# An attention and mixture-of-experts kernel: the whole program as a graph that a list scheduler orders, and a cosine without absolute value

## The chip, the cores and the metric

The kernel runs on one core of one Trainium2 chip. The metric is the device time of one execution in microseconds; of several executions the median counts. The core has five queues that matter here: TensorE (PE in the rows; its weight loads are PEld), VectorE (DVE), ScalarE (ACT), GpSimd (POOL) and SyncE (SP), which issues the DMAs.

## What is computed

Three stages follow one another: attention with keys and values pooled by 8, a dense layer pair with g = h·cos(h), and a mixture of 8 experts whose gate is normalised in 8 Sinkhorn rounds.

```python
def _moe_ref(x, w_in, w_out):
    h = x @ w_in                      # x 2304x512, w_in 512x2048
    g = h * np.cos(h)
    return (g @ w_out).astype(np.float32)

def _moe2_ref(x, w_gate, w1, w2):
    ...                               # P: 2304x8, 8 rounds of row and column sums
    for e in range(E):                # 8 experts, w1 512x1024, w2 1024x512
        h = np.maximum(x @ w1[e], 0.0)
        ye = h @ w2[e]
        out += P[:, e:e + 1] * ye
```

The two weights of the dense pair reach the kernel as 64-bit floats, two 32-bit words each, and become 32-bit floats on the chip.

## The kernel before

Every matmul operand is split into a high half in the reduced format fp32r and the low remainder, and each product is three matmuls: high·high, high·low, low·high (`mm3`). ScalarE writes the high half as a copy; VectorE or GpSimd subtracts it for the low half. What GpSimd can take is a choice of the code, engine by engine.

**Attention and the dense pair (0 to about 540 us).** The 2304 tokens are six blocks of 384 (NB), in the groups [0..3] and [4, 5]; the 2048 hidden columns are four units of 512. `hidden1` (L374 to L392) makes one hidden tile of 128x384: 12 matmuls into the bank `ph`, then ScalarE rounds h/2π to an integer k (L384), VectorE forms r = h - 2πk (L385), ScalarE takes |r| (L387) and sin(π/2 - |r|) (L388), VectorE multiplies by h (L389), ScalarE copies the high half gh (L391), and GpSimd (first group) or VectorE (second) subtracts for gl (L392). 96 such tiles are made. `output1` (L395) multiplies by w_out and adds to `acc` in SBUF (L416, L418); from it come the high and low halves of the next input (L420, L421).

In the first unit `convert` (L108) makes 32 pieces of 128x512 from the 64-bit words: an absolute value on ScalarE (L118), five operations on VectorE (L119 to L127), the add on GpSimd (L128, `cw`); it stores the 32-bit result, and `split` (L93) halves it. For other units and the second group `load_unit` (L100) loads the 32-bit weights, 512 KB a time, and splits them anew: a ScalarE copy (L96) and a GpSimd subtraction (L97) each. The pooling sums of keys and values (`kr`, `ks`, `vr`, `vs`, L202 and L204) stand on GpSimd, except for the first batch; the softmax is on VectorE (L299, L336, L337) and ScalarE. The order of this part follows from that in which the code stands, with lists of attention and conversion tasks worked off between the tiles.

**Mixture of experts (from about 540 us).** Two blocks of tokens make a pair; there are three pairs, and 16 steps (8 experts, two halves of 512 columns each) per pair. The first layer of a step is always a Strassen-Winograd product in two half steps of seven products, P1, P5, P6, P2, P7, P3, P4 (`first_layer` L864, matmuls at L860, six of 384 columns each). Its banks are px (P1, then P2), pv (P5, then P3) and py: when py has been read, ScalarE copies P1's result into it (L879), and P6, P7 and P4 add to it. In pair 0 the second layer is plain (`plain_layer`, L1015, groups of 24 matmuls of 256 columns, `po`), while GpSimd, VectorE and ScalarE form the weight pieces of the Strassen products (L639 to L771) and store them. In pairs 1 and 2, 32 steps, the second layer is Strassen-Winograd too (`strassen_layer`, L1033, banks pc and qc). Its left operands come from `strassen_result` (L912): per half step a sum `spare` on VectorE (L961), three differences `sf` on GpSimd (`combine`, L638), and for seven operands the halves gh (ScalarE) and gl (VectorE). `accumulate` (L993) weighs the result with the gate and adds it (`acc`, L1011). P4 of the second layer may only be added to a qc bank when VectorE has read it (L1066).

The order here is written out by hand: strings such as `"aa0a1a0a1a0a..."` set TensorE's sequence (a: a first-layer product; L or a digit: a piece of the second layer), and a plan with allowances (`later`, `tick`, `until`) puts the other engines' work between. SyncE's DMAs are not in that order.

Of the kernel before, what the change touches and what calls it, by code (L numbers as in the profile page):

```python
# [56 lines left out]

@with_exitstack
def fused_kernel(ctx: ExitStack, tc: tile.TileContext, qT, kT, vT, v0, wa1, wb1, wa2, wb2, wg, out):
    nc = tc.nc  # L60

    const = ctx.enter_context(tc.tile_pool(name="const", bufs=1))
    xp = ctx.enter_context(tc.tile_pool(name="xp", bufs=1))
    wp = ctx.enter_context(tc.tile_pool(name="wp", bufs=19))
    gfirst = ExitStack()
    rawp = gfirst.enter_context(tc.tile_pool(name="rawp", bufs=3))
    gp = gfirst.enter_context(tc.tile_pool(name="gp", bufs=6))
    banks = ExitStack()
    ps_h = banks.enter_context(tc.tile_pool(name="ps_h", bufs=2, space=bass.MemoryType.PSUM))
    ps_o = banks.enter_context(tc.tile_pool(name="ps_o", bufs=2, space=bass.MemoryType.PSUM))  # L70
    ps_s = banks.enter_context(tc.tile_pool(name="ps_s", bufs=2, space=bass.MemoryType.PSUM))
    ps_a = banks.enter_context(tc.tile_pool(name="ps_a", bufs=2, space=bass.MemoryType.PSUM))


# [3 lines left out]
    ident = const.tile([P, P], F32, name="ident")  # L78
    make_identity(nc, ident)


    marks = {}

    @contextmanager
    def behind(engine):
        if engine in marks:
            with tc.issue_after(marks[engine].ins):
                yield
        else:
            yield  # L90


    def split(src, lo_engine, pool=None):  # L93
        hi = (pool or wp).tile([P, FU], F32R, tag="w", name="whi")
        lo = (pool or wp).tile([P, FU], F32R, tag="w", name="wlo")
        nc.scalar.activation(out=hi, in_=src, func=AF.Copy)  # L96
        lo_engine.tensor_tensor(out=lo, in0=src, in1=hi.bitcast(F32), op=ALU.subtract)  # L97
        return hi, lo

    def load_unit(src, u, lo_engine):  # L100
        parts = []
        for j in range(2):
            raw = rawp.tile([P, 2, FU], F32, tag="raw", name="raw")
            nc.sync.dma_start(out=raw, in_=src[u, :, 2 * j:2 * j + 2, :])
            parts += [split(raw[:, i, :], lo_engine) for i in range(2)]
        return parts

    def convert(raw, keep, u, j):  # L108

        words = raw.bitcast(I32).rearrange("p (n w) -> p n w", w=2)  # L110
        high, low = words[:, :, 1], words[:, :, 0].bitcast(U32)
        m = cv.tile([P, FU], I32, tag="m", name="m", bufs=2)
        w = cv.tile([P, FU], F32, tag="cw", name="cw", bufs=2)
# [12 lines left out]
        v.tensor_scalar(out=w.bitcast(I32), in0=m, scalar1=-2**23, scalar2=None, op0=ALU.bitwise_and)
        v.scalar_tensor_tensor(out=w, in0=low, scalar=2.0**-52, in1=w, op0=ALU.mult, op1=ALU.mult)  # L127
# [1212 lines left out]
```

## Time and profile before

| | |
|---|---|
| three runs, us | 2015.01, 2014.88, 2011.66; median 2014.88 |
| profiled execution, us | 2012.12, span 2010.4, granted clock 0.99 |
| TensorE busy | 1955.4 us, 97% of the span, 13220 matmuls |
| VectorE, ScalarE, GpSimd busy | 67%, 49%, 38% |
| chain that ended last | TensorE 67% |
| HBM traffic | 317 MB read, 134 MB written |

The profile shows one execution. A busy share is an average over stages that differ; so it is read by windows, each with the engines' busy time in it and TensorE's granted clock as a share of its full 2.4 GHz. A group of instructions is a line, an engine, an operation and a tile, with the mean time of one. A wait names what ended it.

### The profile page before, as it was taken

The numbers are of one execution on the slowest core, as the hardware profiler recorded it, in microseconds if no ns is written. First come the engines' busy times: TensorE is split into PE (matmuls) and PEld (weight loads), VectorE is DVE, ScalarE is ACT, GpSimd is POOL, SyncE is SP. The second block draws the span as 40 slices with busy tenths as digits, with TensorE's granted clock in tenths as the row PEclk, the third lists the DMA queues.
The fourth block names the chain that finished last, engine by engine and source line by source line (L and its number), as shares of the span: only waits on it lengthen the run. The fifth ranks groups of instructions, "written<-read, shape, count | busy, mean of one in ns | idle before, by whom it ended". The sixth has DMA issues, their size and how long they took to land.

```text
span 2010.4 us, 36447 instructions
## 1 busy us (share of the span) xinstructions
PE 1955.4 (97%) x13220; PEld 1917.9 (95%) x13220; DVE 1354.3 (67%) x2282; ACT 988.4 (49%) x2133; POOL 765.2 (38%) x643
## 2 busy tenths in 40 slices
PE   6799999999989999999999999999999999999999
PEld 4689899999989999999999999999999999999999
DVE  8988776655587676676765566666667656656665
ACT  5676566655534344444434444444445444444443
POOL 7755654432574454344442222122124222212212
PEclk8899999999999999999999999999999999999999
DMA  7533431211688888889897677677668767767763
GB/s 252 153 125 116 126 121 53 83 54 45 222 290 292 310 305 302 298 300 310 306 315 260 236 266 257 229 258 272 232 237 285 245 238 273 248 233 259 268 226 120
DMA packets 257460, 453.33 MB, mean 225 GB/s; under 512 B 25568, under 2 KB 86752, under 8 KB 257280
## 3 DMA queue, kind: packets, MB, share of 16 engines
q1 hardware_dynamic: 257280, 451.01, 65.8%
q8 instruction: 104, 1.70, 0.3%
q14 instruction: 76, 0.62, 0.1%
HBM read 317.21 MB, written 133.69 MB: 224 GB/s over the span
## 4 chain that ended last, share of the span: by engine, by line
PE 67%; DVE 2%; issue 1%; DMA 1%; POOL 1%; ACT 1%; SPq 0%; DVEq 0%; POOLq 0%; ACTq 0%
PE py L860 14%; PE pc L1043 13%; PE po L1025 11%; PE qc L1043 10%; PE pv L860 9%; PE px L860 9%; DMA raw<-wb 1%; DVE gl L646 1%; POOL t L639 0%; DVE vlo L646 0%; DMA w2c<-vhi 0%; POOL vlo L646 0%; DVE gl L840 0%; POOL wlo L646 0%; DVE acc L1011 0%
## 5 line engine op out<-in xcount | busy, mean ns | idle before, releaser
L639 POOL TENSOR_TENSOR sf<-spare 128x384 f32<-128x384 f32 x64 | 66.0, 1032 | 702.3 <-DVE spare L961 702.3
L1043 PE MATMUL pc<-wc,gh 128*128 128x256 f32 x1536 | 284.0, 280 | 0.0
L1043 PEld LDWEIGHTS pc<-wc,gh 128*128 128x128 f32 x1536 | 241.1, 188 | 0.0
L860 PE MATMUL py<-xc,wc 128*128 128x384 f32 x1152 | 232.2, 336 | 0.3 <-DVE pv L886 0.3
L1043 PE MATMUL pc<-wc,gl 128*128 128x256 f32 x768 | 215.6, 281 | 1.1 <-DVE gl L646 1.1
L1043 PE MATMUL qc<-wc,gh 128*128 128x256 f32 x1152 | 215.7, 280 | 0.2 <-DVE pc L1062 0.2
L860 PEld LDWEIGHTS py<-xc,wc 128*128 128x128 f32 x1152 | 193.1, 188 | 0.6 <-DVE pv L886 0.6
L1043 PEld LDWEIGHTS qc<-wc,gh 128*128 128x128 f32 x1152 | 191.6, 188 | 0.9 <-DVE pc L1062 0.6
L1043 PE MATMUL qc<-wc,gl 128*128 128x256 f32 x576 | 162.2, 282 | 0.4 <-DVE gl L646 0.4
L860 PE MATMUL pv<-xc,wc 128*128 128x384 f32 x768 | 155.3, 337 | 2.8 <-DVE gl L840 2.8
L1025 PE MATMUL po<-vlo,gh 128*128 128x256 f32 x768 | 153.0, 281 | 2.3 <-POOL vlo L646 2.3
L646 DVE TENSOR_TENSOR gl<-sf,gh 128x384 fp32r<-128x384 f32 x256 | 148.5, 619 | 9.8 <-ACT gh L652 9.8
L860 PE MATMUL px<-xc,wc 128*128 128x384 f32 x768 | 154.7, 336 | 0.0
L1025 PE MATMUL po<-vhi,gh 128*128 128x256 f32 x768 | 152.4, 280 | 0.0
L1025 PE MATMUL po<-vhi,gl 128*128 128x256 f32 x768 | 152.3, 280 | 0.0
L1043 PEld LDWEIGHTS pc<-wc,gl 128*128 128x128 f32 x768 | 145.1, 189 | 1.3 <-DVE gl L646 1.3
L137 PE MATMUL ph<-xh,whi 128*128 128x384 f32 x384 | 131.2, 346 | 5.9 <-DVE r L389 5.9
L860 PEld LDWEIGHTS pv<-xc,wc 128*128 128x128 f32 x768 | 130.6, 188 | 3.1 <-DVE gl L840 3.1
L138 PE MATMUL ph<-xl,whi 128*128 128x384 f32 x384 | 131.3, 342 | 0.7 <-DVE xl L370 0.7
L860 PEld LDWEIGHTS px<-xc,wc 128*128 128x128 f32 x768 | 130.7, 188 | 0.0
L886 DVE TENSOR_TENSOR pv<-py,s 128x384 f32<-128x384 f32 x96 | 54.2, 564 | 113.5 <-ACT gh L652 87.9
L138 PE MATMUL po<-gl,whi 128*128 128x384 f32 x384 | 129.5, 338 | 0.8 <-POOL gl L392 0.8
(206 smaller groups left out, 5162.8 us busy)
## 6 DMA issues: line engine op xcount, KB each, us to landing
wc<-w1c SPq DMA_DIRECT2D x448, 256.0 KB, 4.7
wc<-w2c SPq DMA_DIRECT2D x448, 256.0 KB, 5.3
w1c<-whi SPq DMA_DIRECT2D x112, 256.0 KB, 4.4
w1c<-wlo SPq DMA_DIRECT2D x112, 256.0 KB, 3.1
w2c<-vhi SPq DMA_DIRECT2D x112, 256.0 KB, 3.8
w2c<-vlo SPq DMA_DIRECT2D x112, 256.0 KB, 2.6
raw<-wa SPq DMA_DIRECT2D x48, 512.0 KB, 5.9
raw<-wb SPq DMA_DIRECT2D x48, 512.0 KB, 4.1
```

The costliest lines, as they stand in the source:

```text
L137: nc.tensor.matmul(out=ps, lhsT=lh, rhs=rh, start=(i == 0), stop=False)
L138: nc.tensor.matmul(out=ps, lhsT=lh, rhs=rl, start=False, stop=False)
L639: nc.gpsimd.tensor_tensor(out=out, in0=x, in1=y, op=op)
L646: e.tensor_tensor(out=lo(), in0=src, in1=high.bitcast(F32), op=ALU.subtract)
L860: nc.tensor.matmul(out=ps, lhsT=l[:, k], rhs=r[:, c, :], start=(start and c + n == 0), stop=(c + n == 3), skip_group_check=True)
L886: nc.vector.tensor_tensor(out=s["v"], in0=ps, in1=s["s5"], op=ALU.add)
L1025: nc.tensor.matmul(out=po[:, d * HD:(d + 1) * HD], lhsT=l[:, r], rhs=w[f % 2, d][k][:, (f // 2) * HD:(f // 2 + 1) * HD], start=(f + n + d ...
L1043: nc.tensor.matmul(out=ps, lhsT=l[:, r], rhs=m[:, k], start=(start and g + n == 0), stop=(g + n == 3), skip_group_check=True)
```

## The change

Every operation becomes a node of one graph: an engine (or two to choose from), planned microseconds, the buffers it reads and writes, and for matmuls a due time. A list scheduler walks through planned time and picks for each engine, among the nodes that could start first, the one whose due time is nearest; SyncE's DMAs are ordered in the same way. TensorE's due times in the experts' part come from the same strings as before.

```diff
-        marks["act"] = nc.scalar.activation(out=k, in_=ps, func=AF.Copy, scale=1.0 / (2.0 * math.pi))
-        nc.vector.scalar_tensor_tensor(out=r, in0=k, scalar=-2.0 * math.pi, in1=ps, op0=ALU.mult, op1=ALU.add)
-
-        nc.scalar.activation(out=r, in_=r, func=AF.Abs)
-        nc.scalar.activation(out=r, in_=r, func=AF.Sin, scale=-1.0, bias=math.pi / 2.0)
+        activate(NB, lambda: r.tile.bitcast(I32), ps, reads=[bank], writes=[r], from_psum=True,
+                 scale=1.0 / (2.0 * math.pi), bias=0.25)
+        add("V", two(NB), lambda: nc.vector.scalar_tensor_tensor(
+            out=r.tile, in0=r.tile.bitcast(I32), scalar=-2.0 * math.pi, in1=ps(), op0=ALU.mult, op1=ALU.add), [bank], [r])
+        activate(NB, lambda: r.tile, lambda: r.tile, AF.Sin, writes=[r], table="sin", bias=math.pi / 2.0)
...
-        nc.gpsimd.tensor_tensor(out=w, in0=mf, in1=w, op=ALU.add)
-        nc.sync.dma_start(out=keep[u, :, j, :], in_=w)
-        return w
+        tt(VG(FU), lambda: w.tile, mf, lambda: w.tile, ALU.add, [m], [w])
+        parts = [buf(k_w if u == 0 else k_cs, [P, FU], F32R, "wc") for _ in range(2)]
+        halves(FU, lambda: w.tile, w, lambda k: parts[k].tile, parts)
+        for k in range(2):
+            load(lambda k=k: wac[u, i, k], lambda k=k: parts[k].tile.bitcast(F32), P * FU * 4, reads=[parts[k]],
+                 writes=[kept_wa[u, i, k]])
+        return parts
...
+    def tt(how, out, in0, in1, op, reads, writes):
+
+        def run(e="V"):
+            (nc.gpsimd if e == "G" else nc.vector).tensor_tensor(out=out(), in0=in0(), in1=in1(), op=op)
+
+        return add(how["engine"], how["us"], run, reads, writes, port=how.get("port", False))
...
+            node.run(e) if len(node.engine) > 1 else node.run()
...
-    def combine(out, x, y, op):
-        nc.gpsimd.tensor_tensor(out=out, in0=x, in1=y, op=op)
-        return out
+        def gsum(out, x, y, reads, writes):
+            return tt({"engine": "G", "us": pool(NB), "port": True}, out, x, y, ALU.subtract, reads, writes)
...
-    with tc.manual_schedule(engines={E_.PE, E_.Activation, E_.DVE, E_.Pool}):
...
+    with tc.manual_schedule(engines={ENGINES.PE, ENGINES.Activation, ENGINES.DVE, ENGINES.Pool, ENGINES.SP}):
+        g.schedule()
```

- The rounding constant 0.25 moves k so that the sine's argument r + π/2 stays within its range without |r|: 96 ScalarE operations fewer.
- The converted weights are halved once and stored as two halves (64 stores of 256 KB in the place of 32), and loaded as halves (112 loads of 256 KB in the place of 28 of 512 KB); 32 ScalarE copies and 32 GpSimd subtractions fall away.
- `VG` marks operations that the scheduler may put on VectorE or on GpSimd: weight adds and low halves, pooling sums, gl, weight pieces. It plans so that a GpSimd operation and a VectorE operation marked `port` (operands in SBUF) don't overlap. The first copy to `acc` may be on ScalarE or VectorE. `hidden1` has three banks for `ph`.
- A node with one engine calls `run` without it, and `tt` then takes VectorE: so the `gsum` nodes, planned as GpSimd's, stand on VectorE.
- The matmuls are the same in number and size. VectorE has 2627 instructions instead of 2284, ScalarE 2004 instead of 2111, GpSimd 254 instead of 648, SyncE 1727 instead of 1595.

**GpSimd at the start**, from its first softmax product (`at`) on. Before:

```order
L299 TENSOR_TENSOR at<-at,rs 128x288
L128 TENSOR_TENSOR cw<-m,cw 128x512
L299 TENSOR_TENSOR at<-at,rs 128x288 x2
L202 TENSOR_TENSOR kr<-kr 128x288
L299 TENSOR_TENSOR at<-at,rs 128x288
L97 TENSOR_TENSOR wlo<-cw,whi 128x512
L202 TENSOR_TENSOR kr<-kr 128x288
L202 TENSOR_TENSOR kr<-kr 128x144
L202 TENSOR_TENSOR kr<-kr 128x288
L202 TENSOR_TENSOR kr<-kr 128x144
L204 TENSOR_TENSOR ks<-kr 128x72
```

Now:

```order
L449 TENSOR_TENSOR at<-at,rs 128x288
L449 TENSOR_TENSOR kr<-kr 128x288 x2
L449 TENSOR_TENSOR kr<-kr 128x144
L449 TENSOR_TENSOR ks<-kr 128x72 x3
L449 TENSOR_TENSOR vr<-vr 72x512 x3
L449 TENSOR_TENSOR vr<-vr 72x256 x2
L449 TENSOR_TENSOR vs<-vr 72x128 x2
L449 TENSOR_TENSOR vr<-vr 72x256
L449 TENSOR_TENSOR cw<-m,cw 128x512
L449 TENSOR_TENSOR vr<-vr 72x512
L449 TENSOR_TENSOR wc<-cw,wc 128x512
L449 TENSOR_TENSOR vr<-vr 72x256
```

Weight adds and low halves (`cw`, `wlo`) stood between the pooling sums; now the sums come first, and one `cw` and one low half (`wc`) stand among the first twelve rows. Up to the 430th matmul, seven of ten `cw` and five of ten low halves stand on VectorE.

**VectorE in a Strassen step**, from the sum `spare` of a half step on. Before:

```order
L961 SCALAR_TENSOR_TENSOR spare<-pv_17698,c_17802 128x384
L1011 SCALAR_TENSOR_TENSOR acc_12611<-qc,pr,acc_12611 128x512
L646 TENSOR_TENSOR gl<-spare,gh 128x384
L646 TENSOR_TENSOR gl<-c_17802,gh 128x384
L646 TENSOR_TENSOR gl<-sf,gh 128x384 x3
L886 TENSOR_TENSOR pv_17889<-py,s_17896 128x384
L646 TENSOR_TENSOR gl<-sf,gh 128x384
L1062 TENSOR_TENSOR pc<-qc,t_17923 128x256
L941 SCALAR_TENSOR_TENSOR gl<-px_17870,gh 128x384
```

Now (the lines are those of the changed kernel; L1209 is `spare`, L1251 `acc`):

```order
L1209 SCALAR_TENSOR_TENSOR spare<-pv_16153,c_16247 128x384
L449 TENSOR_TENSOR gl<-c_16247,gh 128x384
L449 TENSOR_TENSOR sf<-spare 128x384
L1251 SCALAR_TENSOR_TENSOR acc_12583<-pc,pr,acc_12583 128x512
L449 TENSOR_TENSOR qc<-qc,t_16207 128x256
L449 TENSOR_TENSOR sf<-spare,sf 128x384
L449 TENSOR_TENSOR gl<-spare,gh 128x384
L449 TENSOR_TENSOR gl<-sf,gh 128x384
L1251 SCALAR_TENSOR_TENSOR acc_12724<-qc,pr,acc_12724 128x512
L449 TENSOR_TENSOR sf<-sf 128x384
```

Three differences `sf` stand among them, the first two ahead of the next gl of `spare`; `acc` and the qc sum stand behind the first.

**TensorE at the start of a plain step**, from the first layer's second product (P5, bank pv) on. Before (left out: the rest of the 24 `po` matmuls):

```order
L860 MATMUL pv_8246<-xc,wlo 128x384
L1025 MATMUL po<-vhi,gh 128x256 x2
L1025 MATMUL po<-vlo,gh 128x256 x2
L1025 MATMUL po<-vhi,gl 128x256 x2
L1025 MATMUL po<-vhi,gh 128x256 x2
...
L1025 MATMUL po<-vhi,gl 128x256 x2
L860 MATMUL py<-xc,whi 128x384 x2
L860 MATMUL py<-xc,wlo 128x384
```

Now (L1148 are the first layer's matmuls):

```order
L1148 MATMUL pv_8216<-xc,whi 128x384 x2
L1148 MATMUL pv_8216<-xc,wlo 128x384
L1148 MATMUL pv_8216<-xc,whi 128x384 x2
L1148 MATMUL pv_8216<-xc,wlo 128x384
L1148 MATMUL py<-xc,whi 128x384 x2
```

The group of the second layer (`po`) that stood between P5 and P6 (py) has gone from there; P6 follows P5.

## Rows read from the trace of the kernel before

**Rows 1.** The windows view: window: us, busy us of each engine (instructions), clock, DMA.

```profile
30.00:130.00 100.00, 81.81 (x460) 69.66 (x459) 95.83 (x168) 64.60 (x111) 73.62 (x78) 0.88 0.52 160
130.00:500.00 370.00, 362.50 (x2108) 350.24 (x2107) 253.40 (x445) 224.92 (x450) 173.50 (x144) 1.00 0.26 85
500.00:605.00 105.00, 95.48 (x584) 92.38 (x583) 72.38 (x140) 48.45 (x98) 70.09 (x53) 0.97 0.75 253
600.00:1000.00 400.00, 399.65 (x2892) 399.04 (x2892) 282.04 (x410) 176.64 (x344) 181.50 (x130) 1.00 0.88 302
1030.00:1055.00 25.00, 21.83 (x151) 21.11 (x151) 18.83 (x20) 8.89 (x16) 16.65 (x8) 0.93 0.90 310
1050.00:1500.00 450.00, 449.70 (x3207) 449.39 (x3206) 274.27 (x478) 203.42 (x481) 100.04 (x90) 1.00 0.74 254
```

**Rows 2.** TensorE's waits, 30:130, 130:540 and 540:640: us, times, longest.

```profile
PE psc L279 <- DVE at L337: 6.0, 2, 5.6
...
PE ph L137 <- DVE r L389: 4.8, 6, 1.5
...
PE po L1025 <- POOL vlo L646: 2.3, 1, 2.3
```

**Rows 3.** GpSimd's groups by shape, 30:130: busy us, mean ns, idle before.

```profile
L128 POOL TENSOR_TENSOR cw<-m,cw 128x512 f32<-128x512 f32 x10 | 13.9, 1389 | 7.6 <-DVE cw L127 7.6
...
L202 POOL TENSOR_TENSOR vr<-vr 72x512 f32<-72x512 f32 x8 | 10.6, 1325 | 3.0 <-DMA vr<-vt 3.0
...
L204 POOL TENSOR_TENSOR ks<-kr 128x72 f32<-128x72 f32 x9 | 5.0, 560 | 0.1
```

**Rows 4.** VectorE's groups by shape, 30:130.

```profile
L299 DVE TENSOR_TENSOR at<-at,rs 128x288 f32<-128x288 f32 x20 | 17.5, 925 | 0.1
L123 DVE SCALAR_TENSOR_TENSOR m<-raw,m 128x512 int32<-128x512 int32 x10 | 10.3, 1039 | 0.0
...
L337 DVE TENSOR_TENSOR at<-psc,mx 128x288 f32<-128x288 f32 x20 | 8.6, 441 | 0.0
...
L126 DVE TENSOR_SCALAR cw<-m 128x512 int32<-128x512 int32 x10 | 7.3, 743 | 0.0
...
L119 DVE TENSOR_SCALAR m<-m 128x512 f32<-128x512 f32 x8 | 6.4, 800 | 0.1
L121 DVE TENSOR_SCALAR m<-m 128x512 int32<-128x512 int32 x8 | 6.4, 795 | 0.0
```

**Rows 5.** VectorE's groups by shape, 565:1040.

```profile
L646 DVE TENSOR_TENSOR wlo<-raw,whi 128x512 fp32r<-128x512 f32 x65 | 73.0, 1122 | 0.0
...
L646 DVE TENSOR_TENSOR wlo<-s,whi 128x512 fp32r<-128x512 f32 x26 | 17.7, 680 | 0.0
...
L1004 DVE TENSOR_TENSOR acc<-po,acc 128x512 f32<-128x512 f32 x6 | 4.1, 688 | 4.6 <-PE po L1025 4.6
...
L1149 DVE TENSOR_SCALAR acc<-acc,pr 128x512 f32<-128x512 f32 x6 | 2.5, 472 | 0.0
```

**Rows 6.** ScalarE's groups by shape, 0:565.

```profile
L387 ACT ACTIVATE r<-r 128x384 f32<-128x384 f32 x96 | 49.6, 521 | 37.4 <-DVE r L385 36.3
...
L384 ACT ACTIVATE r<-ph 128x384 int32<-128x384 f32 x96 | 46.1, 485 | 57.7 <-PE ph L139 54.7 <-POOL gl L392 2.6
```

**Rows 7.** VectorE's groups by shape, Strassen steps, 1100:1500.

```profile
L646 DVE TENSOR_TENSOR gl<-sf,gh 128x384 fp32r<-128x384 f32 x108 | 61.1, 605 | 4.2 <-ACT gh L652 4.2
L1011 DVE SCALAR_TENSOR_TENSOR acc<-pc,pr,acc 128x512 f32<-128x512 f32 x39 | 29.2, 750 | 10.4 <-PE pc L1043 10.4
...
L1066 DVE TENSOR_TENSOR qc<-qc,t 128x256 f32<-128x256 f32 x40 | 17.3, 432 | 3.0 <-PE qc L1043 0.2
...
L961 DVE SCALAR_TENSOR_TENSOR spare<-pv,c 128x384 f32<-128x384 f32 x28 | 15.6, 557 | 14.8 <-PE pv L860 14.8
```

**Rows 8.** TensorE's timeline from 1200 us: start us, us, instruction.

```profile
1201.23 1.21 PE L860 MATMUL py<-xc,wc 128*128 128x384 f32 x6
1202.28 0.40 PE L1043 MATMUL qc<-wc,gh 128*128 128x256 f32 x2
```

More of the change, by code (lines that the diff above doesn't have):

```diff
@@ L2 @@
 import struct
[L3 removed]
+from contextlib import ExitStack
 import concourse.bass as bass
@@ new lines, with __init__, __getitem__ @@
+class Kind:
+    def __init__(self, group, pool, slots, strict=False):
+        self.group, self.pool, self.slots, self.strict = group, pool, slots, strict
+        self.queue = []
+class Buf:
+    def __init__(self, kind, shape, dtype, name, tile=None):
+        self.kind, self.shape, self.dtype, self.name, self.tile = kind, shape, dtype, name, tile
+        self.acc, self.left, self.slot, self.end = [], 0, None, 0.0
+    def __getitem__(self, key):
+        return self.tile[key]
+class Node:
+    __slots__ = ("engine", "us", "run", "succ", "wait", "new", "bufs", "port", "table", "size", "goal", "late", "est", "slots",
+                 "end", "done", "name")
@@ L71, in fused_kernel @@
-    ps_s = banks.enter_context(tc.tile_pool(name="ps_s", bufs=2, space=bass.MemoryType.PSUM))
-    ps_a = banks.enter_context(tc.tile_pool(name="ps_a", bufs=2, space=bass.MemoryType.PSUM))
+    g = Graph(ctx, tc)
+    add, buf = g.add, g.buf
+    base = g.group("base")
+    first = g.group("first")
+    second = g.group("second")
+    early = g.group("early", "right")
+    mid = g.group("mid", "right", (early,))
+    late = g.group("late", "right", (second,))
+    plain = g.group("plain", "left", (second,))
@@ L193, in fused_kernel, with fill @@
[L193 to L206 removed]
+    def fill(b, hp, ks, ks_ap):
         kbd = kbds[b % 2]
@@ new lines, in fused_kernel, with prime @@
+    g1 = {}
+    x_op = x_pieces(0)
+    for j in range(NBLK):
+        logits(j, clock["t"] - 24.0 + 4.5 * j)
+    primes = [buf(b_y, [P, 512], F32, "pset"), *(buf(b_q, [P, 512], F32, "pset") for _ in range(2))]
+    def prime():
+        for t in primes:
+            nc.tensor.matmul(out=t.tile, lhsT=wg2[:, 0, :], rhs=wg2.tile.rearrange("p c n -> p (c n)"), start=True, stop=True)
+    node = pe(0.7, prime, [wg2], primes, goal=clock["t"] - 5.0)
+    for other in g.nodes:
+        if other is not node and any(b.kind in (b_a, b_o, b_s0) for b in other.new):
+            other.succ.append(node)
+            node.wait += 1
```

1884 lines of the change are left out of this document (965 added, 919 removed).

## Prediction

> **What bounds the kernel now.** I read first the windows by stage, since an average over the span mixes stages with different limits. From 600 us on TensorE is full: 399.65 of 400 us, and 449.70 of 450 in the Strassen steps, at granted clock 1.00 [rows 1]. No matmul is added or removed, so after 600 us the change can save next to nothing; it can only cost there. What can be saved lies in four places of the same view. From 30 to 130 us TensorE is busy for 81.81 of 100 us at clock 0.88: 18.2 us idle, and 81.8 x 0.12 = 9.8 us of low clock. From 130 to 500 us it idles 7.5 us, from 500 to 605 us 9.5 us and 95.5 x 0.03 = 2.9 us of clock, at 1030 to 1055 us 3.2 and 1.5 us [rows 1]. That is 52.6 us, and the clock falls only where TensorE also idles.
>
> Second, who is full where TensorE idles: from 30 to 130 us VectorE works 95.83 of 100 us [rows 1]. The chain of waits says the same: the score bank is awaited from VectorE's subtraction (6.0 us), then the bank ph of `hidden1` from the product r (4.8 us in six waits), then one low half from GpSimd (2.3 us) [rows 2]. So the start is VectorE's, and what the change puts on VectorE there counts in full.
>
> Third, what one operation costs on either engine. The add of a 128x512 weight is 1389 ns on GpSimd [rows 3]; VectorE's ops of that size on free ports are 680 to 688 ns with two inputs and 472 ns with one [rows 5]. The same ops are longer while GpSimd is busy: 1122 instead of 680, and at the start 925 ns for a 128x288 op whose neighbour of that size, reading PSUM, takes 441 [rows 4, 5].
>
> **The change part by part.** The sum is made against the profiled execution, 2012.1 us, which is 2.8 us below the median of the three runs.
>
> T1, start. By the new order 12 ops of 128x512 (7 weight adds, 5 cuts) and 15 pooling sums of six shapes (the largest 1325, the smallest 560 ns [rows 3]) go from GpSimd to VectorE before the 430th matmul. Off GpSimd: 12 x 1.389 + 11.9 = 28.6 us. Onto VectorE: 12 x 0.688 = 8.3 [rows 5], and the sums at the same ratio (0.688/1.389) 5.9; four accumulator copies of 0.55 go to ScalarE, -2.2. Net +12.0 us of work on the engine that bounds. Against it stands relief. From 30 to 130 us the contended groups hold, above their prices on free ports, 20 x (0.925-0.441) + 10 x (1.039-0.680) + 10 x (0.743-0.472) + 8 x (0.800-0.472) + 8 x (0.795-0.472) = 21.2 us [rows 4, 5], beside 73.6 us of GpSimd work [rows 1]: 0.29 us for each. In proportion the 28.6 us take 8.2 with them: net +3.8. If the planner, which never books a GpSimd op beside a VectorE op of this kind, frees all of it: 12.0 - 21.2 = -9.2. I take the middle, **-3**; ends -9 and +12.
>
> How much comes back is where the Trainium skill speaks, and for the change. Its page "SBUF — State Buffer", section "Who interferes with whom", says that a VectorE op with two SBUF inputs and a GpSimd op that reads SBUF take turns at one shared port, and that the one that comes second is blocked. The trace agrees on which ops grow (the 925 and 1122 rows, not the PSUM reader of 441), but by 0.29 us per us of GpSimd, not by 1. By the full rule T1 would be 12.0 - 28.6 = -17 and the forecast 14 us lower.
>
> T2, the dense pair (130 to 500 us). The absolute value is gone: 96 ScalarE ops of 521 ns, 49.6 us [rows 6], each of them in the chain from the last matmul of a bank to r that TensorE waits for [rows 2]. ScalarE also loses 32 copies and gains 19 accumulator copies. The cosine's rounding constant costs no instruction. The halves kept in DRAM take 32 weight cuts off GpSimd; they add 84 loads and 32 stores, where DMA is busy 26% [rows 1]. A chain 0.5 us shorter, and a third bank, cover most of six waits that sum to 4.8: **-4**, ends 0 and -7.5.
>
> T3, into the experts (500 to 605 us). Loss 12.4. GpSimd holds 70.1 us in 53 ops, VectorE 72.4 of 105 [rows 1]. About half of GpSimd's ops move: 26 x 0.69 = 18 us more on VectorE, less 0.29 x 35 = 10 of relief: 80 of 105. The last waits are on GpSimd's slow pieces (2.3 us [rows 2]), which shorten, but the chain of the gate is VectorE's own. **-4**, ends +5 and -10.
>
> T4, switch to Strassen (1030 to 1055 us): 4.7 lost; **-3**. At the worst the new order has seven ScalarE copies ahead of the one that P6 needs, so some 2 us remain. Ends 0 and -4.7.
>
> T5, Strassen steps, 32 of them. The plan books the three differences of a half step (sf) on GpSimd, but the order has them on VectorE, and GpSimd empty. So the change does not do here what its plan says. VectorE gains 6 x 0.557 = 3.3 us of a step of about 29.3, from 61% [rows 1] to 72%, less what the sums gl<-sf (605) win back. The tightest place: from the end of P3 TensorE has 12 products of 256 columns and 12 of 384 to do. Six of 384 take 1202.28 - 1201.23 = 1.05 us [rows 8], so 0.175 each, and by columns 0.117 for 256: 1.40 + 2.10 = 3.50 us. VectorE does spare 0.557, gl<-c 0.557, a difference 0.557, acc 0.750, then the qc add 0.432 [rows 7]: 2.85, with 0.2 of signals 3.05. Slack 0.45 us, so **0**; the upper end is one difference exposed in every half step, 64 x 0.557 = 35.6.
>
> T6, plain steps, 16 of them. VectorE takes some 5.6 ops more per step, 3.9 us of 31.4: from 282.0/400 = 70% [rows 1] to about 80%. P6 now follows P1 and P5 at the step's start, without the group of 24 output products that stood between. Its bank must be read by ScalarE (0.485 [rows 6]) and VectorE (0.557), then filled from P1 (0.485): 1.5 and signals, some 2.0 us, against 12 x 0.175 = 2.1 us of P1 and P5. Slack about 0.1: any late VectorE shows. I take a third of the steps late by one VectorE op, 16/3 x 0.69: **+4**; ends 0 and 16 x 0.69 = 11.
>
> Placing the DMA queue by plan changes no transfer beyond those of T2; I cost it at nothing, as the Strassen steps hold 74% and the plain ones 88% DMA [rows 1] in both. If that cover goes, a late weight load stops TensorE directly; it would show as waits on DMA.
>
> Sum: -3 - 4 - 4 - 3 + 0 + 4 = -10, so 2002.1 us for an execution like the profiled one, and **2005** for the median.
>
> **The rivals.** R1, *the holes close*: the contention goes altogether and the planned order fills T2 to T4: -9 - 7.5 - 10 - 4.7 + 0 = -31, median 1984. For it: 40.4 us of idle and low clock in T1 and T3 whose named waits are all on VectorE or GpSimd, and a planner that sees the whole program. Against it: VectorE still carries more. By its rule of the shared port the Trainium skill ("SBUF — State Buffer", "Who interferes with whom") leans to this side; 0.29 us per us in the trace does not.
>
> R2, *the differences on VectorE stand ahead of the sum that TensorE waits for*: slower. Its place is the qc add before P4 in each half step, its price 0.557 x 64 = 35.6 us, the point from which it decides is VectorE reaching "spare" more than 0.45 us late. For it: the new order does place sf ahead of acc and qc. Against it: VectorE is at 72% only, and TensorE now waits nowhere in this stage. Median 2005 + 36 = 2041; with half of the half steps, 2023.
>
> R3, *no change*: what VectorE takes over weighs what is freed: T1 +4, T2 -4, T3 and T4 0, T6 0 to +4: 2015 to 2019.
>
> **How the numbers follow.** Forecast 0.42, by itself 1993 to 2013; R1 0.22; R3 0.14; R2 0.22. The range reaches over R1's figure and halfway to R2's worst: 1980 to 2034, leaving out about 0.06 below and 0.12 above. A measurement here tells 0.2%, 4 us: faster is below 2010.9, slower above 2018.9. Faster: nine tenths of the forecast (0.38) and R1, 0.60. Same: the rest of the forecast (0.04) and most of R3 (0.10), 0.14. Slower: R2 and the rest of R3, 0.26.
>
> **What would show it.** T1: VectorE's weight ops at the start near 0.7 us instead of 0.8 to 1.04, and TensorE's idle time from 30 to 130 us below 18; if those ops stay long and the idle grows, T1 has the wrong sign. T2: no waits of ph on r. T3, T4: windows 500 to 605 and 1030 to 1055 with less idle. T5: VectorE near 72% in the Strassen steps, GpSimd at zero, TensorE without waits; waits of qc or pc on VectorE speak for R2. T6: py waiting for ScalarE's copy at starts of plain steps. I am wrong altogether if TensorE idles after 600 us for a transfer, or if the start gets longer because a planned order holds a ready instruction behind a late one.

## The result, and the profile after

The changed kernel takes 1991.69 us (median of 4 runs, 1989.5 to 1994.68) against 2014.95 us before: ratio 0.9887, 95% interval 0.9867 to 0.9908. It is faster by 23 us, inside the stated range but by more than double the 10 us that were forecast.

The profiled execution after took 1993.46 us, its span 1991.7, 1.8 us above its median, where the one before was 2.8 us below its own. So the two traces differ by 18.7 us of span; the other 4.6 us are the choice of executions, and only the 18.7 can be traced to places. For that I take marks: the time at which TensorE has begun a given number of matmul columns (the second operand's, 4.159 million in the whole program, the same in every kernel here but for order). The table is worked out from the start of each matmul in the traces; a stretch is the us between two marks.

| stretch, million columns | before | after | difference | term of the forecast |
|---|---|---|---|---|
| 0 to 0.2 (start) | 155.8 | 156.1 | +0.3 | T1 -3 |
| 0.2 to 1.0 (dense pair) | 383.5 | 377.8 | -5.7 | T2 -4 |
| 1.0 to 1.5 (into the experts) | 244.7 | 240.9 | -3.8 | T3 -4, T6 |
| 1.5 to 2.0 (plain steps) | 227.1 | 227.1 | 0.0 | T6 +4 |
| 2.0 to 2.5 (switch) | 234.3 | 227.9 | -6.4 | T4 -3 |
| 2.5 to 4.0 (Strassen steps) | 688.2 | 683.8 | -4.4 | T5 0 |
| 4.0 to the end | 76.9 | 78.2 | +1.3 | T5 0 |

The windows view after, as [rows 1] (window: us; busy us and instructions of TensorE, its weight loads, VectorE, ScalarE, GpSimd; granted clock; DMA share; GB/s):

```profile
30.00:130.00 100.00, 81.56 (x460) 71.09 (x460) 88.58 (x164) 63.77 (x105) 51.52 (x60) 0.89 0.56 175
130.00:500.00 370.00, 365.32 (x2143) 356.58 (x2143) 269.55 (x503) 185.51 (x365) 79.92 (x72) 1.00 0.47 153
500.00:605.00 105.00, 100.09 (x636) 97.10 (x635) 80.84 (x140) 47.17 (x90) 29.21 (x20) 0.97 0.73 251
600.00:1000.00 400.00, 398.64 (x2887) 397.42 (x2886) 310.69 (x497) 176.73 (x344) 102.42 (x72) 1.00 0.88 300
1030.00:1055.00 25.00, 25.00 (x193) 25.00 (x192) 17.00 (x26) 7.50 (x16) 2.38 (x2) 1.00 0.95 341
1050.00:1500.00 450.00, 450.00 (x3209) 449.02 (x3209) 298.39 (x581) 218.47 (x491) 5.40 (x3) 1.00 0.73 254
```

From 30 to 130 us TensorE is where it was, 81.56 us at clock 0.89 (81.81 at 0.88 before), though VectorE has come down from 95.83 to 88.58 and GpSimd from 73.62 to 51.52. From 130 to 605 us TensorE gains 2.8 and 4.6 us. The window of the switch is full, at clock 1.00, and GpSimd has left the Strassen steps. VectorE is busy for 310.69 of 400 us in the plain steps instead of 282.04: 78%, nearly the 80% of the forecast.

VectorE's groups by shape after, 565 to 1040 us (mean ns of one behind the busy us), as [rows 5]:

```profile
L449 DVE TENSOR_TENSOR wlo<-raw,whi 128x512 fp32r<-128x512 f32 x50 | 40.2, 817 | 0.0
L449 DVE TENSOR_TENSOR vlo<-t,vhi 128x512 fp32r<-128x512 f32 x52 | 35.9, 696 | 1.7 <-ACT vhi L442 0.7
...
L449 DVE TENSOR_TENSOR wlo<-s,whi 128x512 fp32r<-128x512 f32 x26 | 18.9, 725 | 1.5 <-ACT whi L442 0.8
```

The low halves wlo<-raw and vlo<-t, 1122 and 1034 ns before, take 817 and 696, which leaves VectorE room for the added work. The start of a plain step after, where the forecast had P6 wait for its bank (start us, us, engine, instruction, idle time before and what ended it):

```profile
699.32 0.33 PE L1148 MATMUL px<-xh,wlo 128*128 128x384 f32 x1
...
699.69 0.47 ACT L442 ACTIVATE py<-px 128x384 f32<-128x384 f32 x1 [2.31 <-PE px L1148]
...
700.54 0.51 PE L1148 MATMUL py<-xc,whi 128*128 128x384 f32 x2
```

ScalarE's copy into py starts when P1's last matmul ends (699.65), not when the bank has been read: its last reader was done 0.97 us earlier. The copy ends at 700.17, 0.37 us before P6 begins. From 775 to 1002 us (the stretch from 1.5 to 2.0 million columns) this copy is made 15 times. In 4 of them P6 follows P1 and P5 directly, with the same 0.37 us and the bank read 2.8 us before the copy. In the other 11 a group of 24 output products still stands between P1 and P6, and P6 begins 2.7 to 2.9 us behind the copy. So the order shown above for the start of a plain step is that of the lesser part of them.

In the Strassen steps, 1100 to 1500 us, as [rows 7]:

```profile
L449 DVE TENSOR_TENSOR gl<-sf,gh 128x384 fp32r<-128x384 f32 x105 | 56.7, 551 | 24.2 <-ACT gh L442 24.2
L1251 DVE SCALAR_TENSOR_TENSOR acc<-pc,pr,acc 128x512 f32<-128x512 f32 x42 | 31.4, 747 | 5.9 <-PE pc L1287 5.9
...
L449 DVE TENSOR_TENSOR qc<-qc,t 128x256 f32<-128x256 f32 x42 | 17.8, 423 | 0.0
...
L1209 DVE SCALAR_TENSOR_TENSOR spare<-pv,c 128x384 f32<-128x384 f32 x28 | 15.6, 558 | 33.6 <-ACT sf L442 33.6
...
L449 DVE TENSOR_TENSOR sf<-spare 128x384 f32<-128x384 f32 x27 | 15.0, 556 | 0.5
```

The differences sf are there, 0.55 us each, and gl<-sf has fallen from 605 to 551. VectorE is busy for 298.39 of 450 us there, 66%, where the forecast said 72%. TensorE's waits after, from 30 to 130 us, and from 130 to 540 (us in total, times, longest), as [rows 2]:

```profile
PE po L765 <- ACT wc L442: 7.0, 1, 7.0
PE psc L590 <- DVE at L449: 4.0, 2, 2.6
...
PE ph L765 <- DVE r L449: 1.9, 2, 1.7
```

The waits for the score bank have fallen from 6.0 to 4.0 us, and one of 7.0 us for a converted weight has come. The timeline after shows what stands before it (start us, us, engine, instruction, idle time before):

```profile
77.21 0.95 DVE L655 TENSOR_REDUCE mx<-psc 128x4 f32<-128x288 f32 x2 [2.08 <-PE psc L590]
...
77.68 0.33 PE L766 MATMUL po<-gl,wc 128*128 128x384 f32 x1
77.76 2.15 POOL L449 TENSOR_TENSOR gl<-r,gh 128x384 fp32r<-128x384 f32 x2 [1.23 <-ACT gh L442]
...
78.08 0.98 DVE L723 TENSOR_SCALAR m<-m 128x512 f32<-128x512 f32 x1
...
79.09 1.10 DVE L725 TENSOR_SCALAR m<-m 128x512 int32<-128x512 int32 x1
79.87 2.57 POOL L449 TENSOR_TENSOR vr<-vr 72x512 f32<-72x512 f32 x2
80.23 1.63 DVE L727 SCALAR_TENSOR_TENSOR m<-raw,m 128x512 int32<-128x512 int32 x1
81.96 0.76 DVE L729 TENSOR_SCALAR cw<-m 128x512 int32<-128x512 int32 x1
...
83.12 0.94 DVE L731 SCALAR_TENSOR_TENSOR cw<-raw,cw 128x512 f32<-128x512 uint32 x1
...
85.02 0.63 ACT L442 ACTIVATE wc<-cw 128x512 fp32r<-128x512 f32 x1 [6.93 <-DVE cw L449]
...
85.71 0.69 PE L765 MATMUL po<-gh,wc 128*128 128x384 f32 x1 [6.99 <-ACT wc L442]
...
88.32 0.52 PE L766 MATMUL po<-gl,wc 128*128 128x384 f32 x1
```

VectorE waits 2.08 us for scores, then does the conversion's five operations in 0.98, 1.10, 1.63, 0.76 and 0.94 us beside GpSimd's, and a low clock follows the idle time: the matmuls at 88 us are 0.52 us long, where they were 0.33 at 77.68. In the trace before, such a case stands at the switch (timeline before, 1035 to 1043 us):

```profile
1035.79 4.79 POOL L806 TENSOR_TENSOR x1r<-x1r 128x768 f32<-128x768 f32 x2
...
1037.03 1.86 DVE L646 TENSOR_TENSOR vlo<-t,vhi 128x512 fp32r<-128x512 f32 x1
...
1038.82 2.30 DVE L646 TENSOR_TENSOR vlo<-raw,vhi 128x512 fp32r<-128x512 f32 x1
...
1041.71 0.54 DVE L840 SCALAR_TENSOR_TENSOR gl<-pv,gh 128x384 fp32r<-128x384 f32 x1
...
1042.30 1.81 PE L860 MATMUL pv<-xc,wc 128*128 128x384 f32 x6 [2.78 <-DVE gl L840]
```

Two low halves, 0.68 us on free ports by [rows 5], took 1.86 and 2.30 us beside GpSimd's differences of x, 2.80 us too long, and TensorE waited 2.78.

### The profile page after: what moved, and what is told of

It is laid out like the page before. It is cut to its first block, busy times and chain, and to the rows that moved or that the text cites. A ratio compares the mean times of both kernels' runs of the same rounds, so it can differ in the third digit from the quotient of the medians.

```text
span 1991.7 us, 35651 instructions
## 1 busy us (share of the span) xinstructions
PE 1942.5 (98%) x13220; PEld 1910.8 (96%) x13220; DVE 1427.6 (72%) x2625; ACT 961.4 (48%) x2026; POOL 284.1 (14%) x249
## 4 chain that ended last, share of the span: by engine, by line
PE 93%; DVE 5%; ACT 1%; DMA 1%; issue 0%; SPq 0%; DVEq 0%; ACTq 0%
PE py L1148 15%; PE pc L1287 13%; PE po L1267 13%; PE qc L1287 10%; PE px L1148 10%; PE pv L1148 10%; PE po L765 3%; PE ph L765 3%; PE po L767 3%; PE ph L766 3%; PE ph L767 3%; PE po L766 3%; PE psc L590 1%; DVE at L449 1%; PE ptr L684 1%; PE px L698 1%
## 5 line engine op out<-in xcount | busy, mean ns | idle before, releaser
L1148 PE MATMUL py<-xc,wc 128*128 128x384 f32 x1152 | 232.0, 336 | 0.7 <-ACT py L442 0.7
L1148 PEld LDWEIGHTS py<-xc,wc 128*128 128x128 f32 x1152 | 197.8, 188 | 1.4 <-ACT py L442 0.9
L1287 PEld LDWEIGHTS qc<-wc,gh 128*128 128x128 f32 x1152 | 186.5, 188 | 2.6 <-DVE qc L449 1.7
L449 DVE TENSOR_TENSOR gl<-sf,gh 128x384 fp32r<-128x384 f32 x256 | 137.6, 551 | 58.3 <-ACT gh L442 55.7
L1148 PE MATMUL pv<-xc,wc 128*128 128x384 f32 x768 | 154.6, 336 | 0.0
L1148 PE MATMUL px<-xc,wc 128*128 128x384 f32 x768 | 154.3, 335 | 0.0
L765 PE MATMUL po<-gh,wc 128*128 128x384 f32 x384 | 132.5, 345 | 7.0 <-ACT wc L442 7.0
L765 PE MATMUL ph<-xh,wc 128*128 128x384 f32 x384 | 133.0, 346 | 3.7 <-DVE r L449 3.7
L767 PE MATMUL ph<-xh,wc 128*128 128x384 f32 x384 | 130.8, 341 | 0.8 <-DVE wc L449 0.8
L766 PE MATMUL ph<-xl,wc 128*128 128x384 f32 x384 | 130.8, 341 | 0.1
L767 PE MATMUL po<-gh,wc 128*128 128x384 f32 x384 | 129.8, 338 | 0.8 <-DVE wc L449 0.8
L1148 PEld LDWEIGHTS pv<-xc,wc 128*128 128x128 f32 x768 | 130.4, 188 | 0.0
L1148 PEld LDWEIGHTS px<-xc,wc 128*128 128x128 f32 x768 | 130.2, 188 | 0.0
```

What stands on the lines that cost most here:

```text
L449: (nc.gpsimd if e == "G" else nc.vector).tensor_tensor(out=out(), in0=in0(), in1=in1(), op=op)
L765: nc.tensor.matmul(out=ps, lhsT=lh, rhs=rh, start=(i == 0), stop=False)
L766: nc.tensor.matmul(out=ps, lhsT=lh, rhs=rl, start=False, stop=False)
L767: nc.tensor.matmul(out=ps, lhsT=ll, rhs=rh, start=False, stop=(i == total - 1))
L1148: nc.tensor.matmul(out=ps(), lhsT=l[:, k], rhs=r[:, c, :], start=(start and c + n == 0), stop=(c + n == 3), skip_group_check=True)
L1287: nc.tensor.matmul(out=ps, lhsT=l[:, r], rhs=m[:, k], start=(start and h + n == 0), stop=(h + n == 3), skip_group_check=True)
```

## The experiments

Sixteen kernels ran. Four questions: what the differences' engine is worth, what the cosine, the weights and the DMA order are worth, what the planner's rule about GpSimd is worth, and what the choice of engine is worth. Each ratio is to runs of the kernel before made beside that kernel. In the table at the end the stretches stand together.

**The differences on GpSimd, as planned.**

```diff
-        def run(e="V"):
+        def run(e=how["engine"] if how["engine"] == "G" else "V"):
```

> The changed kernel with the 192 Strassen differences issued on GpSimd, as its plan books them; the planned order stays the same. Relief theory (the change gains where GpSimd stops lengthening VectorE's operations): gl<-sf goes back from 551 toward 605 to 620 ns, the Strassen steps give back 3 to 5 us, 1995 to 1997. Rival (the sums on VectorE are a load that the steps just carry): VectorE falls from about 66% to 58% there, the waits of qc on VectorE (1.1 us) go, 1989 to 1991. If neither engine matters there: 1991 to 1993.

Measured 1992.86 us, 0.9894 (0.988 to 0.9907). Half of the relief theory is right: gl<-sf is 657 and gl<-spare 968 ns long. But the Strassen steps take 684.0 us against 683.8. So VectorE carries either, the lengthened halves or the added differences.

**The same move in the kernel before**, the three differences on VectorE (`combine(..., nc.vector)`).

> The kernel before with the 192 differences on VectorE alone. Relief theory: gl<-sf falls from 619 to 550, gl<-spare from 857 to 550, the loss of 2 us at 1525 us shrinks and TensorE's time per Strassen step falls a little: 2010 to 2013. Rival R2 of the prediction (the differences stand ahead of what TensorE waits for): waits of pc, qc and py on VectorE appear in the Strassen steps, 2018 to 2040.

Measured 2015.69, ratio 1.0009 (1.0001 to 1.0018): no gain. TensorE and ScalarE have the same instructions in the same order as before. The Strassen steps of either pair keep their 228.4 us per half million columns; the switch is 1.4 us shorter, and the half million columns in which the pairs change take 235.6 us instead of 231.3. TensorE's waits there, 1500 to 1560 us:

```profile
PE pc L1043 <- DVE gl L646: 3.5, 1, 3.5
```

Before, that wait was 1.1 us; the granted clock is 0.94 in this window, 1.00 before. This is like rival R2's mechanism, once in the program and not 64 times. That x's pieces and the differences fall together on VectorE there would explain it; this is argued, not shown.

**The absolute value back.**

```diff
-                 scale=1.0 / (2.0 * math.pi), bias=0.25)
+                 scale=1.0 / (2.0 * math.pi))
...
+        activate(NB, lambda: r.tile, lambda: r.tile, AF.Abs, writes=[r])
-        activate(NB, lambda: r.tile, lambda: r.tile, AF.Sin, writes=[r], table="sin", bias=math.pi / 2.0)
+        activate(NB, lambda: r.tile, lambda: r.tile, AF.Sin, writes=[r], table="sin", scale=-1.0, bias=math.pi / 2.0)
```

> The changed kernel with the absolute value back in the cosine: 96 ScalarE operations of 0.52 us more, 50 us in the first 540. Theory T2 (each chain from a bank to r is 0.5 us shorter for it): the waits of ph on r grow from 3.7 us to 6 to 9 and the windows to 500 us lose 3 to 5 us, 1995 to 1997. Rival (three banks and the planned order hide the chain, ScalarE is at 50% there): within 1.5 us of the changed kernel, 1990 to 1993.

Measured 1996.23, 0.9907 (0.9893 to 0.992): 4.5 us above the changed kernel's median, with intervals that overlap. The dense pair takes 381.5 us instead of 377.8. The waits of ph on r grew only from 1.9 to 2.8 us, not to 6 to 9: the loss is spread, and the theory's sign for it was wrong. Nor is the operation alone in it. With 96 nodes more the planner makes another order, TensorE's from about the 110th matmul on; and two other orders with the new cosine, those of the two tries for a better start below, take 375.3 and 381.5 us there. So up to 3.7 of the 5.7 us can be the cosine's; how many are is open.

**The kernel before without absolute value** (the same edit in `hidden1`).

> The kernel before with the cosine without absolute value alone. The same edit taken back in the changed kernel cost 4.5 us (1996.2 against 1991.7). If it is worth the same here: 2010 to 2012, the six waits of ph on r (4.8 us) mostly gone. If the order written by hand can't use it: 2013 to 2015.

Measured 2018.16, ratio 1.0024 (1.0013 to 1.0034): slower than before. 38 us of ScalarE work are gone from 130 to 500 us (187.22 instead of 224.92), and the dense pair takes 386.1 us instead of 383.5. So ScalarE was not what bound there. The order that follows from the code came out differently too, TensorE's from about the 130th matmul on. In the order made by hand the edit does not pay.

**The weights kept whole** (stored as one 32-bit piece, loaded and halved again).

> The changed kernel with the dense pair's weights kept whole and split anew after each load, as before: 32 more ScalarE copies and 32 more subtractions on VectorE or GpSimd, 84 loads and 32 stores fewer. If the kept halves are worth something, it is from 130 to 500 us, where TensorE loses 4.7 us now: up to 3 us slower, 1993 to 1996. Rival (DMA space and engines are free there): 1990 to 1993.

Measured 1991.43, 0.9894 (0.9881 to 0.9908): no difference. **The DMAs out of the written order** (`ENGINES.SP` taken out of the list):

> The changed kernel with SyncE's DMAs not in the written order. If their planned place is worth something: waits on DMA appear, at the start above all, 1994 to 2005. If transfers are hidden anyway (prediction: costed at nothing): 1990 to 1994.

Measured 1994.74, 0.9904 (0.9881 to 0.9927): 3 us above, with intervals that overlap; TensorE waits on a DMA for 9.7 us in the first 60 us (8.6 in the changed kernel), and later for 0.7 us in all. Whether the planned order of the DMAs is worth anything stays open.

**A planner that lets GpSimd and VectorE overlap.**

```diff
-                    if (e == "G" or (e == "V" and node.port)):
-                        start = max(start, port)
...
-                        if o == "G" or node.port and o == "V":
-                            other = max(other, port)
```

> The changed kernel with a planner that lets GpSimd and VectorE operations on SBUF overlap. If the exclusion matters on the chip: VectorE's weight operations at the start and the plain steps' low halves get longer again, and 3 to 10 us come back, 1995 to 2002. Rival (what was moved off GpSimd decides, not the exclusion): 1990 to 1994.

Measured 2054.23, 1.0201 (1.0187 to 1.0215): 62 us above the changed kernel, far beyond what either side expected, and slower than before. All stretches lose, by the traces: 13 us at the start, 7 in the dense pair, 7 in each of the next two, 25 in the switch and the Strassen steps. Part of that could be the wrong engine of the differences, so **the same with the differences on GpSimd**:

> The planner without the exclusion (2054.2 us), but with the differences really on GpSimd. In that run the Strassen steps (from 2.0 to 4.0 million matmul columns) took 936.7 us against 911.7 in the changed kernel. If this is rival R2 (the plan thinks VectorE free while the differences run on it; the exclusion had reserved that time): the Strassen steps come back to 911 to 918, TensorE's waits for pc and qc go, and the total falls to 2028 to 2038. If it is the lock itself that the plan no longer avoids: the Strassen steps stay at 930 or more, with gl<-sf above 600 ns.

Measured 2042.84, 1.014 (1.0122 to 1.0159). The switch and the Strassen steps come to 928.7 us (231.6 + 697.1) from 936.7 (232.3 + 704.4), the changed kernel has 911.7. TensorE and ScalarE have the same order in both, so 8 us were rival R2: the plan thought VectorE free while the differences ran there. The other 17 are left to an order made without the exclusion. In it TensorE waits once in nearly every step for the sum that VectorE puts into pc, in the first run (differences on VectorE) and in the second (on GpSimd, gl<-sf 655 ns). The waits of TensorE and of its weight loads, 1100 to 1990 us, first run:

```profile
PE qc L1283 <- DVE pc L445: 6.6, 28, 1.3
PEld qc L1283 <- DVE qc L445: 10.7, 27, 0.4
```

Second run:

```profile
PE qc L1283 <- DVE pc L445: 7.0, 29, 0.5
PEld qc L1283 <- DVE pc L445: 16.2, 29, 0.8
```

The 10.7 us for the qc sum, which R2 named, are not there in the second run. The wait for the pc sum is there in both; the weight loads' 16.2 us of it come near the 17.

**The differences booked on VectorE** for what they take there (`V(NB)` in `gsum`).

> The changed kernel with the differences booked on VectorE for what they take there. If the plan's wrong booking cost something, the waits of qc and py in the Strassen steps (2 us) go: 1988 to 1991. If the exclusion already kept VectorE's time free: 1990 to 1993.

Measured 1996.21, 0.9915 (0.9899 to 0.993): 4.5 us slower than the changed kernel, against both expectations. The switch and the Strassen steps take 917.3 us (228.6 + 688.7) instead of 911.7. That the wrong booking, some 1 us each on GpSimd with the exclusion, keeps more of VectorE free than the differences need would explain it; this is argued, not shown. Up to the first difference all engines have the same instructions in the same order here, in the run with the differences on GpSimd and in the changed kernel, and their starts took 161.2, 156.1 and 156.1 us. The dense pair took 376.2 to 377.8. The run with the DMAs out of order, whose engines also have the same order, took 152.9 and 379.4. So a start tells nothing below 5 to 8 us, the dense pair nothing below 2 to 3.

**Everything on VectorE** that `VG` leaves to the planner. Seven operations on x of 128x768 stay on GpSimd, all later than 130 us.

> The changed kernel with everything that may stand on VectorE or GpSimd put on VectorE; GpSimd keeps only its fills. If VectorE bounds the start (prediction, T1): 51 us of GpSimd work from 30 to 130 us come to VectorE as about 26, less some 15 of relief, so TensorE loses 5 to 12 us there and some more in the plain steps (VectorE from 78% to about 85%), 2000 to 2010. Rival (the contention costs as much as the work; with GpSimd empty VectorE's operations are all at their short times): 1986 to 1994.

Measured 2008.54, 0.9977 (0.9968 to 0.9987). VectorE's groups from 30 to 130 us:

```profile
L449 DVE TENSOR_TENSOR at<-psc,mx 128x288 f32<-128x288 f32 x18 | 7.8, 452 | 0.3
...
L449 DVE TENSOR_TENSOR at<-at,rs 128x288 f32<-128x288 f32 x18 | 7.3, 451 | 0.2
...
L731 DVE SCALAR_TENSOR_TENSOR cw<-raw,cw 128x512 f32<-128x512 uint32 x7 | 4.7, 687 | 0.1
...
L449 DVE TENSOR_TENSOR cw<-m,cw 128x512 f32<-128x512 f32 x6 | 4.1, 685 | 0.1
L449 DVE TENSOR_TENSOR wc<-cw,wc 128x512 fp32r<-128x512 f32 x6 | 4.1, 682 | 0.0
```

With GpSimd at 0 us in this window all are at their short times, and VectorE is no fuller than in the changed kernel (89.42 us, against 88.58). The start is hardly longer (157.5 against 156.1). The loss is in the dense pair, 389.3 us instead of 377.8, where TensorE waits 7.3 us for r (1.9 in the changed kernel), and in the switch, 230.6 instead of 227.9. **Everything of `VG` on GpSimd,** and the differences:

> The changed kernel with everything that the planner may place on VectorE or GpSimd put on GpSimd, and the differences too: the engines as before, the order planned. Relief theory: VectorE's operations are as long as before (at the start 0.8 to 1.04 us, wlo 1.0 us and more), and the gains from 500 to 605 and from 1030 to 1055 us (5 us each) go: 2003 to 2015, more if GpSimd becomes the bound at the start. Rival (the planned order is what gains, not the engine): 1990 to 1996.

Measured 2017.35, 1.0017 (1.0008 to 1.0026). The start takes 166.0 us, and in the plain steps GpSimd is the bound: the window from 605 to 1000 us has it busy for 357.46 of 395 us and TensorE for 386.13. So this run does not tell the order from the engines.

**The engines as before, the order planned.** Weight adds, halves of the dense pair and sums on GpSimd, gl of the first group too, the experts' halves shared by the old rule, the differences on GpSimd.

```diff
+def PG(n):
+    return {"engine": "G", "us": pool(n), "port": True}
...
-        tt(VG(FU), lambda: w.tile, mf, lambda: w.tile, ALU.add, [m], [w])
+        tt(PG(FU), lambda: w.tile, mf, lambda: w.tile, ALU.add, [m], [w])
...
-            halves(FU, what[1], what[0], lambda k: parts[k].tile, parts)
+            halves(FU, what[1], what[0], lambda k: parts[k].tile, parts, PG(FU) if u < 3 else V(FU))
```

> The changed kernel, each operation that the planner may place on VectorE or GpSimd put where the kernel before has it (the differences on GpSimd too); order and cosine stay the new ones. If the choice of engines brings the gain: VectorE's operations are as long as before, and 10 us or more come back, 2002 to 2015. If the planned order brings it: 1990 to 1997. An even split: near 2000.

Measured 2027.14, 1.0067 (1.0055 to 1.008): 35 us above the changed kernel and 14 above the one before. So the planner's order with the old engines loses; the choice of engines in it brings more than the whole gain. Not tried were the old engines in a plan that lets them overlap, so whether the 14 us are the order's or those of taking turns with so much on GpSimd stays open. The plain steps lose nothing, though their low halves are longer than in the changed kernel (605 to 1000 us; there 814 and 733):

```profile
L453 DVE TENSOR_TENSOR wlo<-raw,whi 128x512 fp32r<-128x512 f32 x62 | 53.3, 887 | 7.6 <-ACT whi L446 7.6
...
L453 DVE TENSOR_TENSOR vlo<-raw,vhi 128x512 fp32r<-128x512 f32 x24 | 22.8, 959 | 0.0
```

**In the first part alone, and in the experts alone:**

> As the run before, in the attention and the dense pair alone (to about 540 us); in the experts the planner chooses. If the choice matters at the start: the mark of 1.0 million columns (533.9 us in the changed kernel) comes 4 to 10 us later, 1996 to 2002. If not: 1990 to 1994.

> As e13, in the experts' part alone. If the choice matters there, it is at the switch (60 us window from 1000 us, where GpSimd's long differences of x lengthen VectorE's) and in the transition from 500 us: 4 to 10 us, 1996 to 2002. If not: 1990 to 1994.

Measured 2007.25 (0.9979, 0.997 to 0.9987) and 2003.89 (0.9957, 0.9945 to 0.997). The first loses in the dense pair: 389.2 us against 377.8. The longest of TensorE's waits there, 130 to 540 us:

```profile
PE ph L769 <- DVE r L453: 10.3, 2, 9.7
```

One wait of 9.7 us for r: from 178 to 188 us VectorE works through two conversions, in operations of up to 1.63 us, before it comes to r. The second loses on the way into the experts: 250.3 us against 240.9. Its waits from 500 to 760 us:

```profile
PE pc L951 <- DVE cs L948: 9.3, 4, 3.6
PE py L1152 <- DVE c L453: 3.8, 1, 3.8
```

The gate's column sums come late from VectorE (0.8 us of such waits in the changed kernel). The switch stays full in both, 60.00 us of 60 from 1000 us, as it does with the old engines throughout: that gain is the order's, not the engines'. The change of pairs does not: the half million columns around it take 230.1 us (230.2 with the old engines throughout) against 228.6 in the changed kernel and 231.3 before.

**Two tries for a better start.** TensorE's operations of the first 100 us planned 1.2 times as long:

> The changed kernel with TensorE's operations of the first 100 us planned 1.2 times as long, which is nearer to what the low clock and the waits make of them (granted 0.89 to 0.92). If the 7.0 us wait of po for a converted weight at 78 us comes from VectorE's operations standing behind a score that the plan expects too early: that wait goes and 3 to 7 us are saved, 1985 to 1989. Rival (the wait only moves, VectorE is the bound of the start): 1990 to 1994.

Measured 1991.39, 0.9888 (0.9873 to 0.9902). The 7.0 us wait is gone. Those of psc (1.1 us in the changed kernel) and for GpSimd's at have come, while that for xl stood at 5.9 us already; over the whole execution:

```profile
PE ptr L686 <- DVE xl L451: 7.1, 3, 2.8
PE psc L592 <- issue: 5.4, 3, 2.4
PE ptr L686 <- POOL at L451: 2.9, 1, 2.9
```

The start takes 156.1 us, as in the changed kernel. Joined with the whole weights and the differences on GpSimd:

> The changed kernel with the slower TensorE in the plan of the start, the weights kept whole and the differences on GpSimd. Each alone made 0 to 1 us of difference; if the starts add up, 1986 to 1990; if the waits only move, 1990 to 1993.

Measured 1996.39, 0.9914 (0.9901 to 0.9928), 1990.15 to 1997.1: no better. In the profiled execution, the fastest of the five, the start takes 149.0 us and the dense pair 381.5, so part of what the start gains there the next stretch loses. No version here is faster than the changed kernel beyond the noise.

The stretches from the traces, one execution each (us; columns as in the first table):

| kernel | 0-0.2 | 0.2-1.0 | 1.0-1.5 | 1.5-2.0 | 2.0-2.5 | 2.5-4.0 | end | span |
|---|---|---|---|---|---|---|---|---|
| before | 155.8 | 383.5 | 244.7 | 227.1 | 234.3 | 688.2 | 76.9 | 2010.4 |
| after | 156.1 | 377.8 | 240.9 | 227.1 | 227.9 | 683.8 | 78.2 | 1991.7 |
| engines as before | 159.4 | 394.0 | 251.4 | 227.1 | 227.8 | 685.6 | 78.3 | 2023.6 |
| so in the first part | 157.7 | 389.2 | 241.5 | 227.1 | 227.9 | 683.8 | 78.2 | 2005.4 |
| so in the experts | 156.2 | 376.2 | 250.3 | 227.1 | 227.7 | 685.3 | 79.1 | 2002.0 |
| all on VectorE | 157.5 | 389.3 | 240.1 | 227.1 | 230.6 | 683.8 | 78.2 | 2006.7 |
| all on GpSimd | 166.0 | 381.4 | 246.8 | 227.7 | 231.0 | 684.3 | 77.8 | 2015.1 |
| overlap allowed | 169.2 | 384.5 | 247.4 | 234.3 | 232.3 | 704.4 | 80.1 | 2052.2 |
| absolute value back | 155.4 | 381.5 | 239.4 | 227.1 | 228.1 | 683.8 | 78.3 | 1993.5 |

## Why the prediction was wrong

The direction and the range held, and so did the kind of gain in part (relief of VectorE through an emptier GpSimd). The size did not: -10 forecast, -23 measured, of which -18.7 can be placed. Two steps failed: the charge for the plain steps (T6), 4 us too dear, and the premise that little can be saved after 600 us (T4, T5), 6.5 us too small. Step by step:

- **T6, the term furthest off** ("a third of the steps late by one VectorE op: +4"). The stretch of plain steps takes 227.1 us before and after, and in every kernel but three: the two without exclusion and, by 0.6 us, the one with everything on GpSimd. The chain behind the "slack about 0.1" was wrong. It put the reading of the bank, 1.0 us, and the filling one behind the other into the time of P1 and P5. In the trace of that stretch the bank is read before P1 ends wherever P6 follows directly, and the copy waits for P1 alone: slack 0.37 us, and 2.7 us or more elsewhere. From 605 to 1000 us TensorE waits for py once, 0.4 us. Shorter VectorE operations are not the reason: with the old engines they are longer (887 and 959 ns instead of 814 and 733), and the stretch takes 227.1 us all the same.
- **"After 600 us the change can save next to nothing"**, the premise of T4 and T5. From the mark of 2.0 million columns on, 9.5 us were saved where T4 and T5 had 3. 5.5 us are the switch, wholly closed where I left 2 us. 2 us are the change of pairs at 1525 us, which I had passed over: TensorE had 58.28 of 60 us there before. 3 us are a pace (see the last section), and 1.3 were lost again at the end. With the old engines in the planned order the switch (227.8) and the pace stay, so these two come from the order, and not by way of contention as T4 and T5 had it. Of the change of pairs little stays (230.2 us, as above): there the choice of engines counts.
- **T1** (-3): +0.3, which one execution of each can't tell from -3. Its premise was not borne out: "what the change puts on VectorE there counts in full". With all such work on VectorE the start took 1.4 us longer, not 5 to 12, and VectorE was busy for 89 us of 100, as in the changed kernel. The start is a chain of single operations on several engines. Where the 7.0 us wait for a weight was taken away, others came up, and the start was no shorter.
- **T2** (-4): -5.7, of which the cosine at most 3.7. The mechanism was only half right: the waits of ph on r fell from 4.8 to 1.9 us, but with the absolute value back they are 2.8, so most of that fall is not the cosine's. In the hand-made order the cosine alone is worth nothing.
- **T3** (-4): -3.8 for the stretch that also holds the first plain steps. It rests on the choice of engines, -9.4 against the planned order with the old ones in the experts.
- **T5 and R2**: the differences on VectorE cost nothing, as forecast. The reason given (0.45 us of slack) is not the whole one. The plan reserves VectorE while it believes GpSimd to be at work, and so leaves the differences their time by accident: without that reservation they cost 8 us, and R2 comes up.
- **R1** (1984) was nearer than the forecast, in part by luck. The contention did not go altogether (817, not 680), and the start gained nothing where R1 had 9 us. What it did not foresee is that the planner's order and its choice of engines need each other: -35 by the choice, +14 by the order with the old engines.

Where the Trainium skill was weighed ("SBUF — State Buffer", "Who interferes with whom"), its direction was right. In the run with GpSimd empty all the two-input operations of 128x512 from 30 to 130 us take 682 to 687 ns and at<-at,rs takes 451 instead of 925, while the PSUM reader of scores takes 441 to 452 ns in seven of the traces, beside GpSimd or not. The -17 us that its full rule gave for T1 did not come; the run with all such work on VectorE suggests that the start does not hang on VectorE's load.

## What to carry to other kernels

When two engines lengthen each other's operations, plan them as taking turns and let the planner choose the engine: here one without the other lost 14 us (old engines) and 28 to 40 us (overlap, with the differences on GpSimd or on VectorE) against the kernel before, and both together won 23. Price a move by what it does to the operations that stay as well as by its own time, and don't take a busy share of 95% for a bound: try the move that should hurt most. And look at every place where an otherwise full engine falters, however short: the switch and the change of pairs held 7.5 of the 18.7 us.

## What was not expected of the hardware

- In the Strassen steps no wait of TensorE is shown before, and yet the planned order is faster there: 227.6 instead of 228.4 us per half million columns. From 1600 to 1900 us a matmul of 256 columns starts behind another of 256 after 117.47 ns on average before and 116.85 after, at full clock in both; the same with the differences on GpSimd (116.86) or, in the old order, on VectorE (117.49). So it goes with the order of the matmuls. The planned order goes from 256 to 384 columns 92 times there where the old one does so 122 times; that this is the cause was not tried, and the pairs averaged here lie within stretches of 256.
- An operation on VectorE can be lengthened by far more than the means show: 1.86 and 2.30 us for one of 0.68, at the switch before, where TensorE waited 2.78 us.
